# One x ring with paced chunk loads, a third product buffer and a second transpose bank in a dynamic convolution with mixture of depths

## The chip, the cores and the metric

One Trainium2 chip, one of its cores. TensorE (PE), VectorE (DVE), ScalarE (ACT), GpSimd (POOL) and SyncE (SP) run their own instructions in order and meet at semaphores. The metric is the device time of one execution in microseconds (us). Where several executions of a kernel are compared, their median is taken.

## What is computed

x is 8 x 4160 tokens of 192 values, weight_gen has 8 heads times 7 taps for each token. Part one is a causal convolution whose weights are a softmax over the 7 taps, for each token and head; part two takes, in each of the 8 sequences, the 128 tokens of the highest score and adds a gated two-layer expert to them:

```python
w = softmax(weight_gen, axis=-1)                      # (B, S, 8, 7)
x_pad = concat([zeros(6), x], axis=1)                 # along the tokens
out[b, s, h] = sum over k of w[b, s, h, k] * x_pad[b, s + k, h]
scores = out @ w_gate
for b in range(8):
    top = the 128 tokens of the highest scores[b]
    ye = relu(out[b, top] @ w1) @ w2                  # 192 -> 1024 -> 192
    out[b, top] += sigmoid(scores[b, top])[:, None] * ye
```

## The kernel before, in words

The 33,280 tokens are cut into 128 runs of 260, one for each partition. Each partition keeps its 260 tokens along the free dimension, and 6 more of the run before as a halo. The 260 are cut into 5 tiles of 52 tokens and 65 sub-steps of 4 tokens (13 a tile). Four tile buffers of x (fp16, converted by the load on POOL's queue, `load_x`, L593) exist; the fifth tile reuses the first.

Everything is emitted in one hand-written order, `phase`, and each engine runs its own instructions in that order. The main loop runs g from 0 to 65. In step g it emits:

- `products(g)`, L762 on VectorE: x of 10 tokens times the doubled weights, 5376 values a partition, written to a buffer of the pool `prodp` (two buffers).
- for each of two halves: a step of `softmax`, of `dots`, of `score`, of the selection, and `tap_sums(g - 1, half)`, L774: seven matmuls against the identity add up the taps of one half in PSUM.
- `store(g - 1)`: ScalarE copies the sums out (L782), SP's queue writes them (L783).

The generators are advanced by `next`, one piece of work for each call. `softmax` works on pieces of the weights: load on SP's queue (`load_wg`, L617, two pieces ahead, buffers shared with the halo), exponential on ScalarE into `e` (L649, three buffers), den by TensorE (L194), inverse by two ScalarE operations (L202, L204), each a call later, and the multiply on VectorE (L635). `dup_weights` (L746, ScalarE) writes each weight twice in a row for the products. `dots` computes x @ w_gate head by head for the scores: eight transposes on TensorE into the one bank `tps` (L697), a ScalarE copy `xT` (L702), eight small matmuls (L683) a call later, and a copy into `y16` (L688). The halo of each next tile is copied from the last (L605). `score` multiplies y with the weights (L719), sums the taps (L726) and reduces (L730).

When all tokens are scored, the selection starts: `threshold_selection` (top-8 of 260 scores, five times, then five rounds of a 15-way threshold search on VectorE and TensorE, then eight indirect loads of the picked list on POOL, L558), then `expert_pass`. That one computes the eight batches' picked rows anew: it gathers the 8 rows' weights (L253) and windows of x (L274, four ahead, and one for the head of the sequence, L279) with indirect loads on POOL, makes their softmax weights (es L295, den, inverse, we L304 and L308, wes L315), and then runs a loop over batches: `tap_rows` (L321), `conv_rows` (L334), `turn_rows` (L346), two `hidden` (L360, L364), `outputs` (L376) and `finish` (L383), a batch every three calls. From `rowf` on (a copy that waits for the picked list) the selection gets a call in both halves of a step, before that in one. At the end the eight batches are scattered into the output one after another (`scatter_rows`, L408): they write the tensor that the 65 stores wrote, and wait for these and for each other.

## Time and profile before

| | |
|---|---|
| median of 2 runs | 427.47 us (427.12 to 427.81) |
| the profiled execution | 424.73 us |
| its span, first to last instruction | 423.0 us |
| TensorE matmuls, busy | 251.7 us (60%) |
| VectorE, busy | 246.5 us (58%) |
| ScalarE, busy | 188.5 us (45%) |
| POOL, busy | 71.0 us (17%) |
| mean granted TensorE clock | 0.883 |
| products that start from 50.72, 151.62, 215.50, 286.02 and 321.02 us on | 12, 15, 13, 7 and 18 |

A busy time is the sum over the instructions of an engine. PE counts matmuls, whose ends are modelled; PEld (weight loads) overlaps with it. "[idle before <- releaser]" behind a row is the time that the engine stood still before it, and what ended that. The granted clock is 1.00 at 2.4 GHz and 0.50 at 1.2 GHz; between these it is a mean over both. GB/s counts the bytes as they land.

### The profile page before, as it was taken

How to read it: one execution, taken by the hardware profiler on the slowest of the kernel's cores; microseconds unless marked ns; L12 is line 12 of the kernel's file. 1: busy time of each engine (PE TensorE's matmuls, PEld its weight loads, DVE VectorE, ACT ScalarE, POOL GpSimd, SP SyncE). 2: the span in 40 equal slices, each digit the busy share in tenths (PEclk: the TensorE clock that was granted, in tenths of full speed). 3: DMA queues.
4: the chain of work that ended last, by engine and by line, in shares of the span. 5: the costliest groups of instructions: out<-in, count | busy, mean ns of one | idle time of the engine just before them, and what ended most of it. 6: DMA issues, size and time to landing. Idle time of an engine off the chain costs nothing. (4 is left out here: it accounts for less than half of the span.)

```text
span 423.0 us, 5356 instructions
## 1 busy us (share of the span) xinstructions
PE 251.7 (60%) x2174; PEld 159.8 (38%) x2174; DVE 246.5 (58%) x224; ACT 188.5 (45%) x244; POOL 71.0 (17%) x75
## 2 busy tenths in 40 slices
PE   0001117656466999799985757646267999996000
PEld 0001115333343666566642323323134777753000
DVE  1000242443435798687899999739529999894000
ACT  2004259656756785878723132204036666642000
POOL 3500000000000030000000000375847630000230
PEclk9999999886987999999998786886869999999555
DMA  8999974422311249921220211112149762224000
GB/s 139 238 244 230 242 212 141 162 93 81 104 69 40 77 110 230 240 113 77 114 113 37 115 74 75 63 52 112 56 84 239 152 174 103 113 112 154 29 28 20
DMA packets 17529, 51.41 MB, mean 122 GB/s; under 512 B 3989, under 2 KB 4379, under 8 KB 16346
## 3 DMA queue, kind: packets, MB, share of 16 engines
q0 software_dynamic: 5040, 17.35, 21.9%
q1 hardware_dynamic: 12458, 33.66, 21.5%
q8 instruction: 19, 0.31, 0.3%
q14 instruction: 12, 0.10, 0.1%
HBM read 41.61 MB, written 26.40 MB: 161 GB/s over the span
## 5 line engine op out<-in xcount | busy, mean ns | idle before, releaser
L762 DVE TENSOR_TENSOR prod<-xt,wd 128x5376 f16<-128x5376 f16 x65 | 191.5, 2954 | 77.5 <-PE cps L774 56.5
L774 PE MATMUL cps<-prod,ident 128*128 128x384 f16 x910 | 186.7, 355 | 27.0 <-DVE prod L762 24.7
L774 PEld LDWEIGHTS <-ident 128*128 128x128 f16 x910 | 90.5, 105 | 96.6 <-DVE prod L762 36.1
L782 ACT COPY co<-cps 128x768 f32<-128x768 f32 x65 | 51.9, 799 | 77.1 <-PE cps L774 62.1
L702 ACT COPY xT<-tps 128x1024 f16<-128x1024 f16 (+3 forms) x52 | 50.7, 975 | 15.2 <-PE tps L697 14.4
L649 ACT ACTIVATE e<-wg_t 128x896 f16<-128x896 f32 (+3 forms) x16 | 29.3, 1830 | 62.7 <-DMA wg_t<-in_weight_gen_dram 47.6
L194 PE MATMUL den<-e,ident 128*128 128x128 f16 (+3 forms) x112 | 11.6, 261 | 70.9 <-ACT lnd L202 66.4
L194 PEld LDWEIGHTS <-ident 128*128 128x128 f16 x119 | 10.4, 121 | 86.8 <-issue 83.5
L697 PE MATMUL tps<-ident,xt 128*128 128x128 f16 x399 | 33.1, 229 | 0.0
L558 POOL DMA_INDIRECT picked<-list_d,at_i x8 | 11.6, 1444 | 113.2 <-DVE flag L567 111.1
L683 PE MATMUL yps<-gmat,xT 128*128 128x8 f16 (+1 forms) x399 | 18.2, 169 | 19.2 <-ACT xT L702 18.8
L593 POOL DMA_DIRECT2D xt<-in_x_dram x11 | 6.2, 578 | 136.6 <-DVE scores L730 135.8
L683 PEld LDWEIGHTS <-xT 128*128 128x128 f16 x399 | 15.0, 98 | 33.2 <-ACT xT L702 32.4
L746 ACT COPY wd<-w 128x1792 f16<-128x1792 f16 (+3 forms) x16 | 27.4, 1710 | 0.0
L697 PEld LDWEIGHTS <-xt 128*128 128x128 f16 x399 | 24.6, 102 | 0.0
L274 POOL DMA_INDIRECT big<-in_x_dram,win_i x8 | 21.8, 2731 | 8.9 <-DVE big L321 7.6
L635 DVE TENSOR_TENSOR w<-e,r 128x896 f16<-128x896 f16 (+3 forms) x16 | 9.9, 627 | 22.3 <-ACT r L204 21.6
L408 POOL DMA_INDIRECT out_dram<-big,row_i x8 | 7.8, 978 | 64.3 <-DMA out_dram<-co 49.4
L253 POOL DMA_INDIRECT wsel<-in_weight_gen_dram,row_i x8 | 15.2, 1900 | 7.4 <-DVE win_i L222 5.3
L719 DVE TENSOR_TENSOR sp<-w,y 128x1344 f16<-128x1344 f16 (+3 forms) x10 | 9.1, 912 | 8.0 <-ACT y L688 8.0
L368 ACT ACTIVATE hT<-hps 128x512 bf16<-128x512 f32 x16 | 9.7, 605 | 6.5 <-PE hps L364 6.2
L831 DVE TENSOR_SCALAR xt<-halo,keep_p 128x1152 f16<-128x1152 f32 x1 | 0.8, 820 | 17.6 <-DMA halo<-in_x_dram 17.6
(130 smaller groups left out, 158.6 us busy)
## 6 DMA issues: line engine op xcount, KB each, us to landing
out_dram<-co SPq DMA_DIRECT2D x65, 384.0 KB, 2.3
xt<-in_x_dram POOLq DMA_DIRECT2D x8, 1248.0 KB, 22.2
wg_t<-in_weight_gen_dram SPq DMA_DIRECT2D x10, 448.0 KB, 7.2
wg_t<-in_weight_gen_dram SPq DMA_DIRECT2D x4, 560.0 KB, 3.6
xt<-in_x_dram POOLq DMA_DIRECT2D x1, 1344.0 KB, 16.4
xt<-in_x_dram POOLq DMA_DIRECT2D x1, 768.0 KB, 9.4
halo<-in_x_dram SPq DMA_DIRECT2D x1, 504.0 KB
xt<-in_x_dram POOLq DMA_DIRECT2D x1, 384.0 KB, 6.4
```

Of the source, the lines that this page charges most:

```text
L194: nc.tensor.matmul(out=den[:, :, :], lhsT=ident16[:, :], rhs=e_k(k), start=(k == 0), stop=(k == K - 1),)
L253: nc.gpsimd.indirect_dma_start(out=wsel[:, b, :], out_offset=None, in_=wg_flat[:, :], in_offset=bass.IndirectOffsetOnAxis(ap=row_i[:, b:b ...
L274: nc.gpsimd.indirect_dma_start(out=win_of(b), out_offset=None, in_=x_elems, in_offset=bass.IndirectOffsetOnAxis(ap=win_i[:, b:b + 1], axis=0),
L558: nc.gpsimd.indirect_dma_start(out=picked[:, b, :], out_offset=None, in_=list_d[:, :], in_offset=bass.IndirectOffsetOnAxis(ap=at_i[:, b:b ...
L649: nc.scalar.activation(out=es[n][:, :, :, :], in_=wgts[n].rearrange("p (s c) h k -> p s k (c h)", c=C), func=AF.Exp)
L683: nc.tensor.matmul(out=o, lhsT=lhs, rhs=m, start=(w == 0), stop=(w == 2), skip_group_check=True,)
L697: nc.tensor.transpose(out=tps[:, j, :], in_=xf[:, (r0 + j) * RUN:(r0 + j + 1) * RUN], identity=ident16[:, :],)
L702: nc.scalar.copy(out=xT[:, 0:m, :], in_=tps[:, 0:m, :])
L746: nc.scalar.copy(out=wd[:, 0:n, :, :, :], in_=w16s[it][:, s0:s0 + n, :, :, None].to_broadcast([P, n, K, CH, 2]),)
L762: nc.vector.tensor_tensor(out=prod.rearrange("p k t (h a b) -> p k t h a b", h=H, b=2), in0=xwin, in1=wd.rearrange("p k (c h) b -> p k c h ...
L774: nc.tensor.matmul(out=cps[:, j, 0:HB], lhsT=ident16[:, :], rhs=pf[:, k, j * HB:(j + 1) * HB], start=(k == 0), stop=(k == K - 1),)
L782: nc.scalar.copy(out=co[:, :, :], in_=cps[:, :, 0:HB])
```

## The change

The tiles of x become one ring of 168 tokens (and 6 of halo) in one buffer, filled by chunks: 8 and 16 tokens first, then 20 or so, each issued on POOL behind a tiny copy that reads the result of the n-th exponential (`after_exp`), the rest when the products of a certain step are emitted. All multiplied weights are kept in one tensor `w16`. Pieces of the weights are one sub-step, then four at a time, loaded three ahead into a pool of their own (three buffers); the halo has a product buffer. `e` has four buffers, `xT` three, `tps` two banks (a pool `ps2`, which the expert's `hps` uses as well), the products three buffers. In `softmax`, den and inverse stand in one call; in `dots`, the small matmuls come two calls behind their transposes. Dots get 0.82 calls a half from step 1 on; the selection starts at a first half. Scores are copied out of PSUM by ScalarE before the reduce. In `expert_pass` the row weights are gathered and made in two halves of four batches, between window gathers, and the loop handles a batch every two calls. The scatter stands inside `phase`, still last.

```diff
-    T = 52
-    NT = SP // T
+    RING = 168
...
+    ps2 = ctx.enter_context(tc.tile_pool(name="ps2", bufs=2, space=PSUM))
...
-        for b in range(NWIN):
-            gather(b)
+        for j in range(2):
+            for b in range(j * B // 2, (j + 1) * B // 2):
+                gather_weights(b)
+            for b in range(j * NWIN // 2, (j + 1) * NWIN // 2):
+                gather(b)
...
+        def row_weights(j):
+            h = slice(j * BH, (j + 1) * BH)
+            nc.scalar.activation(
+                out=es[:, h, :, :],
+                in_=wsel[:, h, :].rearrange("p b (h k) -> p b k h", k=K), func=AF.Exp
+            )
+            den = tap_sum(lambda k: es[:, h, k, :], BH, H)
+            rs = inverse(den, BH, H)
+            nc.vector.tensor_tensor(
+                out=we[:, h, :, :], in0=es[:, h, :, :],
+                in1=rs[:, :, None, :].to_broadcast([P, BH, K, H]), op=MUL,
+            )
...
         for _ in range(GWAIT):
             yield
...
+        row_weights(0)
+        yield
+        yield
+        double(0)
+        row_weights(1)
+        yield
         yield
...
-            tp = ps1.tile([P, 2, P], BF16, tag="tps", name="tp")
+            tp = ps1.tile([P, 2, P], BF16, tag="den", name="tp")
...
-            hps = ps1.tile([P, FC // 2, P], FP32, tag=("den", "sps")[half], name="hps")
+            hps = ps2.tile([P, FC // 2, P], FP32, tag="tps", name="hps")
...
-        for i in range(B + 4):
-            if 0 <= i - 3 < B:
-                finish(i - 3, outputs(i - 3))
+        for i in range(B + 3):
+            if 0 <= i - 1 < B:
+                conv_rows(i - 1)
             if i < B:
                 tap_rows(i)
+            if i == 0:
+                double(1)
             if 0 <= i - 2 < B:
                 hidden(i - 2, 0)
             yield
...
                 hidden(i - 2, 1)
-            yield
-            if i < B:
-                conv_rows(i)
+            if 0 <= i - 3 < B:
+                finish(i - 3, outputs(i - 3))
             yield
...
-        xin = cctx.enter_context(tc.tile_pool(name="xin", bufs=4))
-        xtp = cctx.enter_context(tc.tile_pool(name="xtp", bufs=2))
-        wfull = cctx.enter_context(tc.tile_pool(name="wfull", bufs=4))
-        ep = cctx.enter_context(tc.tile_pool(name="ep", bufs=3))
+        xin = cctx.enter_context(tc.tile_pool(name="xin", bufs=1))
+        xtp = cctx.enter_context(tc.tile_pool(name="xtp", bufs=3))
+        wgl = cctx.enter_context(tc.tile_pool(name="wgl", bufs=3))
+        ep = cctx.enter_context(tc.tile_pool(name="ep", bufs=4))
...
-        prodp = cctx.enter_context(tc.tile_pool(name="prodp", bufs=2))
+        prodp = cctx.enter_context(tc.tile_pool(name="prodp", bufs=3))
...
+        xr = xin.tile([P, RING + PAD, D], FP16, tag="xr", name="xr")
+        w16 = xin.tile([P, NSUB, K, CH], FP16, tag="w16", name="w16")
...
+        pieces = [(0, 1)] + [(a, a + 4) for a in range(1, NSUB, 4)]
...
+        def after_exp(n):
+            nc.gpsimd.tensor_copy(out=tick[:, n:n + 1], in_=es[n][0:1, 0, 0, 0:1])
...
-                j = n - 2
-                if 0 <= j < np_:
-                    rs[j] = inverse(dens[j], pieces[j][2] - pieces[j][1], CH)
                 j = n - 1
-                if 0 <= j < np_:
+                if 0 <= j < NP:
                     e = es[j]
-                    dens[j] = tap_sum(lambda k: e[:, :, k, :], pieces[j][2] - pieces[j][1], CH)
+                    m = pieces[j][1] - pieces[j][0]
+                    rs[j] = inverse(tap_sum(lambda k: e[:, :, k, :], m, CH), m, CH)
...
-                    if n + 2 < np_:
-                        load_wg(n + 2)
+                    if n + 3 < NP:
+                        load_wg(n + 3)
+                    if n in paced:
+                        after_exp(n)
+                        load_x(*paced[n])
...
-            for i in range(len(plan) + 1):
-                if i > 0:
+            for i in range(len(plan) + 2):
+                if i > 1:
...
-                    tps = ps1.tile([P, GRP, P], FP16, tag="tps", name="tps")
+                    tps = ps2.tile([P, GRP, P], FP16, tag="tps", name="tps")
...
-                sps = ps1.tile([P, m, CH], FP32, tag="sps", name="sps")
+                sps = ps1.tile([P, m, CH], FP32, tag="den", name="sps")
...
+                nc.scalar.copy(
+                    out=ss.rearrange("p s (c h) -> p s (c h)", c=C), in_=sps[:, :, :]
+                )
...
+        load_wg(1)
+        load_gate()
+        load_wg(2)
+        load_x(8, 24)
+        edges = [24, 44, 64, 84, 104, 124, 144, RING]
+        paced = dict(enumerate(zip(edges[:-1], edges[1:])))
...
         next(sm)
+        gate_matrix()
...
-        next(sm)
-        dup_weights(0, 0)
-
+        for _ in range(3):
+            next(sm)
+        dup_weights(0)
+
+        late = []
+        for a in range(RING, SP, 20):
+            b = min(SP, a + 20)
+            late.append(((b - RING + PAD - 1) // C + 1, a, b))
...
-                if g < 3 or half == 0:
+                if half == 0 and (g < 8 or g % 3):
                     advance(sm)
-                if g >= DOT0[min(NT - 1, state["block"])]:
-                    advance(dt)
+                if g >= 1:
+                    done_dots += DOTS
+                    if done_dots >= 1:
+                        done_dots -= 1
+                        advance(dt)
...
+            if late and g >= late[0][0]:
+                load_x(*late.pop(0)[1:])
...
-    GWAIT = 6
+    GWAIT = 4
+    DOTS = 0.82
```

## Rows read from the trace of the kernel before

**Rows 1.** By stage: window; its us; busy (count) by engine; clock; DMA share; GB/s.

```profile
0.00:50.72 50.72, 2.34 (x21) 2.01 (x22) 2.63 (x6) 8.88 (x11) 9.25 (x34) 1.00 0.98 217
50.72:151.62 100.90, 63.37 (x632) 42.69 (x632) 49.73 (x46) 65.92 (x83) 0.00 (x0) 0.88 0.36 112
151.62:215.50 63.88, 58.96 (x688) 39.94 (x685) 51.23 (x28) 48.37 (x55) 4.32 (x8) 1.00 0.54 146
215.50:286.02 70.52, 45.49 (x216) 22.35 (x215) 59.35 (x94) 16.14 (x19) 11.56 (x8) 0.81 0.19 74
286.02:321.02 35.00, 18.62 (x91) 9.56 (x91) 22.38 (x19) 11.41 (x16) 23.59 (x13) 0.75 0.40 107
321.02:385.60 64.58, 60.53 (x516) 42.00 (x516) 61.16 (x35) 36.48 (x64) 14.47 (x5) 1.00 0.50 142
385.60:423.00 37.40, 2.45 (x14) 1.29 (x14) 0.00 (x0) 1.31 (x2) 7.82 (x8) 0.59 0.12 44
```

**Rows 2.** Timeline, start: start, us, engine, line, operation [idle before, releaser].

```profile
21.89 0.82 DVE L831 TENSOR_SCALAR xt<-halo,keep_p 128x1152 f16<-128x1152 f32 x1 [17.55 <-DMA halo<-in_x_dram]
...
35.95 1.80 ACT L649 ACTIVATE e<-wg_t 128x896 f16<-128x896 f32 x1 [31.54 <-DMA wg_t<-in_weight_gen_dram]
...
48.46 1.40 ACT L649 ACTIVATE e<-wg_t 128x672 f16<-128x672 f32 x1 [8.11 <-DMA wg_t<-in_weight_gen_dram]
...
50.72 2.96 DVE L762 TENSOR_TENSOR prod<-xt,wd 128x5376 f16<-128x5376 f16 x1 [12.14 <-ACT wd L746]
```

**Rows 3.** Timeline, one step of the slow stage, and two later products.

```profile
118.74 2.96 DVE L762 TENSOR_TENSOR prod<-xt,wd 128x5376 f16<-128x5376 f16 x1 [3.20 <-PE cps L774]
...
121.62 0.62 DVE L635 TENSOR_TENSOR w<-e,r 128x896 f16<-128x896 f16 x1
...
122.27 1.80 ACT L649 ACTIVATE e<-wg_t 128x896 f16<-128x896 f32 x1 [2.15 <-DVE w L635]
123.98 0.99 ACT L702 COPY xT<-tps 128x1024 f16<-128x1024 f16 x1
...
125.69 2.09 PE L774 MATMUL cps<-prod,ident 128*128 128x384 f16 x7
...
127.82 2.96 DVE L762 TENSOR_TENSOR prod<-xt,wd 128x5376 f16<-128x5376 f16 x1 [5.24 <-PE cps L774]
...
137.53 2.88 DVE L762 TENSOR_TENSOR prod<-xt,wd 128x5376 f16<-128x5376 f16 x1
...
155.70 2.96 DVE L762 TENSOR_TENSOR prod<-xt,wd 128x5376 f16<-128x5376 f16 x1 [0.83 <-ACT xT L702]
```

**Rows 4.** Timeline, gathers and row weights after the selection.

```profile
290.78 3.25 POOL L253 DMA_INDIRECT wsel<-in_weight_gen_dram,row_i  x1 [0.30 <-DVE inside L245]
...
303.42 0.94 POOL L253 DMA_INDIRECT wsel<-in_weight_gen_dram,row_i  x1 [0.30 <-issue]
...
312.68 1.02 POOL L279 DMA_INDIRECT big<-xpad,head_i  x1 [4.54 <-issue]
...
318.40 3.54 POOL L274 DMA_INDIRECT big<-in_x_dram,win_i  x1 [0.30 <-issue]
...
321.02 0.85 DVE L321 TENSOR_TENSOR big<-big,wes 128x1344 f16<-128x1344 f16 x1
```

**Rows 5.** Timeline of TensorE in the row loop.

```profile
340.04 1.30 PE L774 MATMUL cps<-prod,ident 128*128 128x384 f16 x7
341.18 0.82 PE L376 MATMUL yep<-w_sb,hT 128*128 128x192 bf16 x8
...
346.83 0.82 PE L376 MATMUL yep<-w_sb,hT 128*128 128x192 bf16 x8
```

**Rows 6.** Timeline, the first and last of eight scatters.

```profile
392.52 1.02 POOL L408 DMA_INDIRECT out_dram<-big,row_i  x1 [49.38 <-DMA out_dram<-co]
...
414.29 0.97 POOL L408 DMA_INDIRECT out_dram<-big,row_i  x1 [2.15 <-issue]
```

More of the change, by code (lines that the diff above doesn't have):

```diff
@@ L251, in expert_pass, with gather_weights @@
         wsel = rowp.tile([P, B, HK], FP32, tag="wsel", name="wsel")
-        for b in range(B):
+        def gather_weights(b):
             nc.gpsimd.indirect_dma_start(
@@ new lines, in row_weights @@
+        def row_weights(j):
[10 more added lines that the diff above has]
+            )
+            nc.vector.tensor_tensor(
+                out=we[:, h, :, :], in0=we[:, h, :, :],
+                in1=inside[:, h, :, None].to_broadcast([P, BH, K, H]), op=MUL,
+            )
@@ L300, in expert_pass @@
-        yield
-        rs = inverse(den, B, H)
-        yield
-        we = rowp.tile([P, B, K, H], FP16, tag="we", name="we")
-        nc.vector.tensor_tensor(
-            out=we[:, :, :, :], in0=es[:, :, :, :],
-            in1=rs[:, :, None, :].to_broadcast([P, B, K, H]), op=MUL,
-        )
-        nc.vector.tensor_tensor(
-            out=we[:, :, :, :], in0=we[:, :, :, :],
-            in1=inside[:, :, :, None].to_broadcast([P, B, K, H]), op=MUL,
-        )
+        row_weights(0)
         yield
@@ L313, in expert_pass @@
         yield
-        wes = rowp.tile([P, B, K, H, 2], FP16, tag="wes", name="wes")
-        nc.scalar.copy(
-            out=wes[:, :, :, :, :], in_=we[:, :, :, :, None].to_broadcast([P, B, K, H, 2])
-        )
+        double(0)
+        row_weights(1)
+        yield
         yield
@@ L601, in new_x @@
-        def new_x():
-            xts.append(xin.tile([P, T + PAD, D], FP16, tag="xt", name=f"xt{len(xts)}"))
-        def halo_copy(it):
-            nc.scalar.copy(out=xts[it][:, 0:PAD, :], in_=xts[it - 1][:, T:T + PAD, :])
-        pieces = [(0, 0, 2), (0, 2, 6), (0, 6, 10), (0, 10, 13)]
-        for it in range(1, NT):
-            pieces += [(it, 0, 4), (it, 4, 8), (it, 8, 13)]
-        wgts = {}
+        xr = xin.tile([P, RING + PAD, D], FP16, tag="xr", name="xr")
+        xflat = xr.rearrange("p t d -> p (t d)")
@@ new lines, in phase, with load_x @@
+        w16 = xin.tile([P, NSUB, K, CH], FP16, tag="w16", name="w16")
+        def load_x(a, b):
+            o = PAD + a % RING
+            nc.gpsimd.dma_start(
+                out=xr[:, o:o + b - a, :],
+                in_=bass.AP(
+                    tensor=x_flat.tensor, offset=x_flat.offset + a * D,
+                    ap=[[SP * D, P], [D, b - a], [1, D]],
+                ),
+            )
+        pieces = [(0, 1)] + [(a, a + 4) for a in range(1, NSUB, 4)]
+        NP = len(pieces)
@@ L613, in load_wg @@
+        wgts, es = {}, {}
         def load_wg(n):
-            it, a, b = pieces[n]
-            m = b - a
-            wg_t = wgp.tile([P, m * C, H, K], FP32, tag="wg", name="wg_t")
+            a, b = pieces[n]
+            wg_t = wgl.tile([P, (b - a) * C, H, K], FP32, tag="wg", name="wg_t")
             nc.sync.dma_start(
@@ L814, in phase @@
             )
-        load_x(0, [8, 24, 52])
-        gate_matrix()
-        for _ in range(3):
-            new_x()
-            load_x(len(xts) - 1, [0, 26, 52])
+        load_wg(1)
[4 more added lines that the diff above has]
+        paced = dict(enumerate(zip(edges[:-1], edges[1:])))
         start_p = scp.tile([P, 1], FP32)
@@ L841, in phase, with advance @@
         dt, sc, sel = dots(), score(), None
-        def advance(gen, n=1):
-            for _ in range(n):
-                next(gen, None)
+        dup_at = {a - 1: n for n, (a, b) in enumerate(pieces) if n}
+        def advance(gen):
+            next(gen, None)
         prods = {}
-        for g in range(NT * NSUB + 1):
-            it, s = divmod(g, NSUB)
-            if g < NT * NSUB:
-                prods[g] = products(it, s)
+        done_dots = 0.0
+        for g in range(NSUB + 1):
+            if g < NSUB:
+                prods[g] = products(g)
@@ L861, in phase @@
                     advance(sel)
                 if half == 0:
-                    s2 = s + 1
-                    if (it, s2) in chunks:
-                        dup_weights(it, s2)
-                    elif s2 == NSUB and it + 1 < NT:
-                        dup_weights(it + 1, 0)
-                    if s == 9 and it + 1 < NT:
-                        halo_copy(it + 1)
+                    if g in dup_at:
+                        dup_weights(dup_at[g])
+                    if g == RING // C - 10:
+                        nc.scalar.copy(out=xr[:, 0:PAD, :], in_=xr[:, RING:RING + PAD, :])
```

184 lines of the change are left out of this document (83 added, 101 removed).

## Prediction

> **What bounds it now.** I began with busy time by stage [rows 1], cut where the character of the loop changes; a "step" is one sub-step g: one product (VectorE, L762) and the tap sums of the product before it. The reader should see that no engine is full on average and that each stage has its own limit. To 50.72 us there is no product, and the DMA share is 0.98. To 151.62: 12 steps of 8.4 us, no engine above 66%. To 215.50: 15 steps of 4.26, TensorE 92% busy. To 286.02: 13 steps of 5.42, VectorE 84%, selection beside the products. To 321.02: 7 steps of 5.0, VectorE 64%. To 385.60: 18 steps of 3.59, VectorE 95%. Then 37.40 us without a product.
>
> Next I read the timeline of the start [rows 2]. Two exponentials wait 31.54 and 8.11 us for weight loads; the halo is there at 21.89, yet the first product starts at 50.72. Four x tiles (208 tokens, 10.2 MB as fp16) are in flight, and 217 GB/s over 50.72 us are 11.0 MB: weights sit behind x.
>
> Third came one whole step of the slow stage [rows 3]. Read it as a ring: product, weight multiply, exponential (which waited 2.15 for the multiply), xT copy, tap sums, next product: 118.74 to 127.82, 9.08 us. Two product buffers, three e buffers and one transpose bank hand each engine its buffer only when the one before is through.
>
> **The change, part by part.** Counted from the loops: 50 dot groups need 52 advances at 1.64 a step (0.82 a half), so dots end in g=32, scoring in g=34, and the selection starts in g=35 instead of 27. It takes 29 steps (13 of threshold, 16 of row work) instead of 38 and ends in g=63, inside the 65 steps: nothing spills behind the loop.
>
> *Start.* A chunk of 20 tokens is 0.98 MB in SBUF, a weight piece of four sub-steps 0.46 MB. The first product needs the fourth exponential, and ahead of its weights stand 44 tokens of x (2.16 MB), halo (0.57) and the pieces (1.49 with its own): 4.2 MB at 217 GB/s are 19.4, plus 1.4 before the first x load: 21 us. Below, 15, if x yields; above, 31: the piece used at 48.46 was loaded behind the exponential that ended near 37.75, so it took 10.7. The gate loads move behind a piece on SP's queue, and gate_matrix, now behind chunk 24 to 44 on POOL, holds chunk 44 to 64 until they land. That delays x, which has slack, and leaves the DMA engines to the weights. The tick copies are one element each; behind one stands only the next x load, on purpose.
>
> *Steps 0 to 7.* The ring is cut at three places: product g waits for tap sums g-3, exponential n for multiply n-4, transposes i for xT i-2, each a step or so old. What is left is each engine's load and the DMA. Up to g=8 the DMA has 8.26 MB of x, 5.2 of weights, 0.57 of halo and 2.8 of stores, 16.8 MB: 78 us at 217 GB/s, so g=8 at 79 at the latest. From below: ScalarE had 65.92 us of work in 12 steps with as many exponentials, 5.5 a step, less 0.36 of a 1.0 us xT copy: 5.1, g=8 at 62. I take 5.8 a step, g=8 at 67.4, nearer the lower end, since the dots are at token 61 by then and the last chunks may still be on their way.
>
> *Steps 8 to 19*, two softmax pieces in three steps. The nearest row is the old loop with its last softmax parts, 137.53 to 155.70, four steps of 4.54 [rows 3]; below, VectorE's own: 2.96, two thirds of 0.62, and 0.37 of scoring (in the third stage VectorE had 3.42 a step, 0.46 above a product, at two groups): 3.7. I take 4.4, as the dots are fewer a step: g=20 at 120.2. *Steps 20 to 34*, no softmax: 4.26 was with two groups and two product buffers [rows 1]; VectorE alone has 3.3, TensorE 3.6 (3.93 a step at two groups, 58.96 over 15). I take 3.8: g=35 at 177.2.
>
> TensorE's clock: the granted clock was 1.00 where TensorE was 92% busy and 0.88 where it was 63% busy [rows 1]; at 125.69 a tap half took 2.09 us [rows 3], at 340.04 1.30 [rows 5]. TensorE's 4 us of work in a 5.8 us step is 70%, later near 90%, so I charge nothing beyond 5.8. The Trainium skill (TensorE: Matmul & The Clock Gate, Part 1: The HAM clock gate) says that the throttled state is the default and that activity lifts it, which speaks against early steps that wait for DMA. By that rule the first eight steps would take about 7.2 each and the sum be 11 us longer; the trace agrees that the clock falls where TensorE waits.
>
> *Selection, 35 to 47.* The threshold code is unchanged and bound by VectorE, 13 steps as before: 70.5, g=48 at 247.7.
>
> *Row weights, 48 to 52.* On POOL a gather issued under a product took 3.25 us, one beside an idle VectorE 0.94, 0.30 apart [rows 4]. The new order is weights 0 to 3, window 0 with its head, window 1, weights 4 to 7, windows 2 and 3. The instructions are the old ones in halves, but exponential, den, inverse and the VectorE multiplies now stand in one call, so VectorE waits for the gathers directly, where it ran out of product buffers before. From the start of product 48: product 2.96, index work 1.3, products 49 and 50, to 10.2 us. Weights 3 is issued at about 12 and landed at 14, plus 2 for the chain to the inverse: VectorE waits 6. Product 51 ends at 19.6. Meanwhile POOL does window 0, its head (which waits 4.54 for the landing [rows 4]) and window 1, to 21.7, then four weights at 1.25, landed at 28.4, plus 2: VectorE waits 11. After product 52 the first tap_rows starts at 35, just as now (286.02 to 321.02), though five products lie before it instead of seven. Bounds: 24 without the second wait, 45 with every gather at 3.25. Behind es on ScalarE stand copy-outs, behind den on TensorE tap sums; both have room before the row loop. g=52 is over at 282.7.
>
> *Row loop.* One batch a step instead of two in three steps. TensorE: a tap half 1.14 (340.04 to 341.18), one batch 5.65 - 3 x 1.14 = 2.23 (341.18 to 346.83) [rows 5], so 4.51 a step; VectorE 2.96, 0.85 and a shorter finish, under 4.4. Products 53 to 64 are five full steps at 4.55, six that fill or drain at 3.3 to 4.2 (22.9), and the last product, 2.95: 48.6, to 331.3. Windows are gathered four batches ahead.
>
> *Tail.* Scatters still follow all stores and each other, 392.52 to 414.29 [rows 6]: the stage stays 37.4, to 368.7.
>
> *Costed at nothing.* The ring spares ScalarE three halo copies, where it isn't the bound. The ss copy, eight times on ScalarE, shares the den bank: a TensorE wait that 4.4 and 3.8 have room for. Late chunks wait on POOL for products, with selection masks, expert weights and, much later, gathers behind them, and are issued five or more steps (20 us) ahead of use. Could a chunk into the one ring tile hold up products on other tokens? Tap_rows at 321.02 ran while a gather into another part of big was still being issued (318.40 plus 3.54) [rows 4], so ranges are told apart. Keeping all weights issues nothing.
>
> The sum: 21 + 46.4 + 52.8 + 57 + 70.5 + 35 + 48.6 + 37.4 = 368.7 against a span of 423.0. The profiled execution is 424.73, so 1.7 lies around it: 370.4. The median of 427.47 is 2.7 above that execution: 373.
>
> **Rivals.** *Weights still late.* The DMA stays full to g=8, which comes at 79, and the ring empties more slowly up to g=20: 385 to 397. For it: a wait of 31.54 behind x now. Against: one chunk for each exponential. Chance 0.2.
> *Cold TensorE.* If the granted clock stays low through the first 20 steps, twice 3.6 is 7.2 a step: +45, 418. Against: a TensorE that is the bound is always busy, and the stage from 151.62 had 1.00. Chance 0.08.
> *The ring survives*, the other side. The inverse now stands in the call of its own den, so ScalarE waits for TensorE before its exponential. If that closes a new ring, the 20 softmax steps keep a length like the old one: at 8.1 a step the time is 436, at 9.08 it is 455. From 8.1 on the change is slower. Against: den is TensorE's first work of a step, on an input a step old. Chance 0.05.
> *More hides*: 3.8 and 3.4 a step in 8 to 34 (-13) and no second wait in the row weights (-11): 349. For it: beside an idle VectorE, POOL runs at 1.25. Chance 0.15.
>
> **How the numbers follow.** My own case has 0.52 and its own range is 356 to 390 (start 15 to 31, g=8 at 62 to 79, row weights 24 to 45, not all at one end). With the late weights above and the better case below the range is 346 to 402, which leaves out about 0.15. Less than 2% either way (419 to 436) is about what can't be told from no change. Faster: my case, the late weights, the better case and part of the cold TensorE, 0.89; the rest of that, 0.06, within; the surviving ring 0.05.
>
> **What would show it.** First product near 21 us; spacing of products near 5.8, 4.4 and 3.8 where it was 8.4 and 4.26; no wait of VectorE for tap sums before g=35; the first top-8 near 181; waits of 6 and 11 us on VectorE for the inverse, about g=51 and 52; spacing near 4.5 in the row loop with TensorE full; the tail at 37.4. I am wrong if steps 0 to 19 keep 8 us, if exponentials still wait for weights after g=8, or if rows finish behind the last product.

## Result and the profile after

The changed kernel takes 378.33 us (median of 2 runs, 377.89 to 378.77) beside 427.47: a ratio of 0.885 [0.880, 0.890]. Forecast were 373 and a range of 346 to 402. The profiled execution took 378.77 us, its span is 377.1, the mean granted clock 0.886.

Busy time by stage of the changed kernel, the view of [rows 1]. The cuts are the starts of products 0, 8, 20, 35 and 48, the end of product 52, and the end of product 64:

```profile
0.00:27.32 27.32, 2.59 (x26) 2.29 (x27) 2.43 (x7) 9.12 (x12) 5.74 (x24) 1.00 0.84 199
27.32:72.43 45.11, 29.99 (x268) 20.36 (x266) 28.66 (x18) 31.31 (x39) 8.15 (x19) 0.89 0.95 247
72.43:136.40 63.97, 51.56 (x604) 37.60 (x602) 44.68 (x39) 50.16 (x65) 4.27 (x8) 0.97 0.62 167
136.40:188.37 51.97, 50.95 (x568) 36.45 (x567) 49.34 (x27) 40.14 (x50) 1.06 (x2) 1.00 0.48 145
188.37:258.42 70.05, 42.73 (x209) 20.80 (x209) 58.71 (x93) 15.28 (x18) 11.94 (x8) 0.87 0.20 74
258.42:291.04 32.62, 14.33 (x63) 6.94 (x64) 16.96 (x20) 9.46 (x17) 17.32 (x13) 0.66 0.44 97
291.04:337.92 46.88, 46.00 (x437) 34.64 (x436) 43.69 (x28) 28.32 (x56) 13.42 (x4) 1.00 0.49 132
337.92:377.10 39.18, 3.24 (x20) 1.75 (x18) 0.00 (x0) 1.60 (x2) 7.83 (x8) 0.60 0.14 52
```

The reader should see two things. The first eight steps are 5.64 us each and the next twelve 5.33, where the first twelve were 8.4. And in the third row no engine is above 81% of 63.97 us, so something other than an engine's load still sets those steps. In the fourth row TensorE has 98%, and that stage has a bound.

By the starts of products, 23.4 us are gained at product 0 (50.72 to 27.32), 53.0 at product 12, 70.7 at product 35 and 66.3 at product 48. Behind it 18.5 are given back: steps 48 to 63 take 76.55 us instead of 58.0, since the selection now starts at step 35 and its row weights and row loop both lie there. The span is 45.9 shorter.

The start, timeline of ScalarE and VectorE, answering [rows 2]:

```profile
18.43 1.80 ACT L660 ACTIVATE e<-wg_t 128x896 f16<-128x896 f32 x1 [14.03 <-DMA wg_t<-in_weight_gen_dram]
...
21.75 1.78 ACT L660 ACTIVATE e<-wg_t 128x896 f16<-128x896 f32 x1
24.52 0.28 ACT L203 ACTIVATE lnd<-den 128x128 f32<-128x128 f32 x1 [0.99 <-PE den L195]
...
25.05 1.78 ACT L660 ACTIVATE e<-wg_t 128x896 f16<-128x896 f32 x1
26.73 0.55 ACT L763 COPY wd<-w 128x448 f16<-128x448 f16 x1
...
27.32 2.96 DVE L778 TENSOR_TENSOR prod<-xr,wd 128x5376 f16<-128x5376 f16 x1 [10.62 <-ACT wd L763]
```

Weights are there at 18.43, for the second exponential, and the two behind it do not wait for theirs; before, exponentials waited until 35.95 and 48.46. But the exponentials then follow each other 3.3 us apart, each behind the den and inverse of the one before, and the doubling of piece 0, whose own exponential was done at 3.5, stands behind all three.

Waits of the changed kernel over the span (engine, line, releaser: us, times, longest):

```profile
DVE prod L778 <- ACT wd L763: 38.7, 10, 10.6
ACT r L205 <- DVE w L647: 18.2, 7, 3.8
ACT e L660 <- DMA wg_t<-in_weight_gen_dram: 18.0, 4, 14.0
DVE we L310 <- ACT r L205: 15.4, 2, 10.2
```

No product waits for tap sums any more, where such waits of 3.20 and 5.24 us stood in [rows 3]. VectorE now waits for the doubled weights, and ScalarE, before it can write an inverse `r`, for a weight multiply. One such turn in steps 9 to 12, timeline of both engines:

```profile
81.04 1.69 ACT L763 COPY wd<-w 128x1792 f16<-128x1792 f16 x1
82.75 2.96 DVE L778 TENSOR_TENSOR prod<-xr,wd 128x5376 f16<-128x5376 f16 x1 [6.83 <-ACT wd L763]
...
86.63 2.95 DVE L778 TENSOR_TENSOR prod<-xr,wd 128x5376 f16<-128x5376 f16 x1
89.50 0.62 DVE L647 TENSOR_TENSOR w<-e,r 128x896 f16<-128x896 f16 x1
90.21 0.31 ACT L205 ACTIVATE r<-lnd 128x128 f16<-128x128 f32 x1 [3.81 <-DVE w L647]
...
98.77 0.31 ACT L205 ACTIVATE r<-lnd 128x128 f16<-128x128 f32 x1 [3.59 <-DVE w L647]
```

`r` has two buffers. The multiply reads `r` two calls after it is written, so the inverse of piece n+2 can only be written when the multiply of piece n is through. That multiply stands behind a product on VectorE, and the product behind a doubling on ScalarE. It is a ring through two engines, smaller than the old one.

Row weights, timelines of POOL and VectorE, answering [rows 4]; and TensorE at the end of the row loop, answering [rows 5]:

```profile
262.66 5.82 DVE L778 TENSOR_TENSOR prod<-xr,wd 128x5376 f16<-128x5376 f16 x2
263.18 3.24 POOL L255 DMA_INDIRECT wsel<-in_weight_gen_dram,row_i  x1 [0.30 <-issue]
266.73 2.57 POOL L255 DMA_INDIRECT wsel<-in_weight_gen_dram,row_i  x1 [0.31 <-issue]
269.61 0.94 POOL L255 DMA_INDIRECT wsel<-in_weight_gen_dram,row_i  x1 [0.30 <-issue]
...
273.66 0.28 DVE L310 TENSOR_TENSOR we<-es,r 128x224 f16<-128x224 f16 x1 [5.18 <-ACT r L205]
...
276.18 1.95 POOL L282 DMA_INDIRECT xr<-xpad,head_i  x1 [4.36 <-issue]
...
287.46 0.28 DVE L310 TENSOR_TENSOR we<-es,r 128x224 f16<-128x224 f16 x1 [10.24 <-ACT r L205]
...
290.95 0.85 DVE L337 TENSOR_TENSOR xr<-xr,wes 128x1344 f16<-128x1344 f16 x1
...
333.51 0.82 PE L392 MATMUL yep<-w_sb,hT 128*128 128x192 bf16 x8
334.17 6.99 PE L790 MATMUL cps<-prod,ident 128*128 128x384 f16 x42
```

The two forecast waits of VectorE are there (5.18 and 10.24 us). In the last row, 3.75 us before the last product ends (at 337.92), TensorE still has 42 matmuls in front of it: six tap halves, or three products.

### The profile page after: what moved, and what is told of

Same layout as the page of the kernel before. It is cut to its first block, busy times and chain, and to the rows that moved or that the text cites. A ratio compares the mean times of both kernels' runs of the same rounds, so it can differ in the third digit from the quotient of the medians.

```text
span 377.1 us, 5393 instructions
## 1 busy us (share of the span) xinstructions
PE 241.4 (64%) x2181; PEld 160.8 (43%) x2181; DVE 244.5 (65%) x225; ACT 185.4 (49%) x255; POOL 69.7 (18%) x85
## 3 DMA queue, kind: packets, MB, share of 16 engines
q1 hardware_dynamic: 12602, 33.66, 23.5%
## 5 line engine op out<-in xcount | busy, mean ns | idle before, releaser
L778 DVE TENSOR_TENSOR prod<-xr,wd 128x5376 f16<-128x5376 f16 x65 | 191.1, 2949 | 38.7 <-ACT wd L763 38.7
L719 ACT COPY xT<-tps 128x1024 f16<-128x1024 f16 (+1 forms) x50 | 50.2, 1012 | 6.5 <-PE tps L715 6.0
L660 ACT ACTIVATE e<-wg_t 128x896 f16<-128x896 f32 (+1 forms) x17 | 29.5, 1738 | 18.0 <-DMA wg_t<-in_weight_gen_dram 18.0
L195 PE MATMUL den<-e,ident 128*128 128x128 f16 (+1 forms) x119 | 11.3, 248 | 37.9 <-ACT e L660 35.1
L195 PEld LDWEIGHTS <-ident 128*128 128x128 f16 x133 | 10.3, 113 | 56.8 <-issue 52.8
L715 PE MATMUL tps<-ident,xr 128*128 128x128 f16 x399 | 32.1, 226 | 0.0
L763 ACT COPY wd<-w 128x1792 f16<-128x1792 f16 (+1 forms) x17 | 27.6, 1623 | 0.0
L715 PEld LDWEIGHTS <-xr 128*128 128x128 f16 x399 | 24.2, 101 | 0.3 <-issue 0.3
L277 POOL DMA_INDIRECT xr<-in_x_dram,win_i x8 | 17.3, 2158 | 7.2 <-DVE xr L337 6.0
L425 POOL DMA_INDIRECT out_dram<-xr,row_i x8 | 7.8, 979 | 54.5 <-issue 48.2
L205 ACT ACTIVATE r<-lnd 128x128 f16<-128x128 f32 (+1 forms) x19 | 5.6, 297 | 18.5 <-DVE w L647 18.2
L736 DVE TENSOR_TENSOR sp<-w,y 128x1792 f16<-128x1792 f16 (+2 forms) x9 | 9.0, 995 | 4.6 <-ACT y L705 4.6
```

Of the source, the lines that this page charges most:

```text
L195: nc.tensor.matmul(out=den[:, :, :], lhsT=ident16[:, :], rhs=e_k(k), start=(k == 0), stop=(k == K - 1),)
L277: nc.gpsimd.indirect_dma_start(out=win_of(b), out_offset=None, in_=x_elems, in_offset=bass.IndirectOffsetOnAxis(ap=win_i[:, b:b + 1], axis=0),
L660: nc.scalar.activation(out=es[n][:, :, :, :], in_=wgts[n].rearrange("p (s c) h k -> p s k (c h)", c=C), func=AF.Exp)
L715: nc.tensor.transpose(out=tps[:, j, :], in_=xflat[:, e0:e0 + RUN], identity=ident16[:, :],)
L719: nc.scalar.copy(out=xT[:, 0:m, :], in_=tps[:, 0:m, :])
L763: nc.scalar.copy(out=wd[:, 0:b - a, :, :, :], in_=w16[:, a:b, :, :, None].to_broadcast([P, b - a, K, CH, 2]),)
```

## Experiments

Each was timed beside the kernel before on the same chip (medians there 427.2 to 429.2 us). Starts of products in each kernel's own profile, in us:

| kernel | time | ratio | p 0 | p 8 | p 20 | p 35 | p 48 | p 64 |
|---|---|---|---|---|---|---|---|---|
| before | 427.5 | 1 | 50.7 | 127.8 | 186.7 | 259.1 | 324.7 | 382.7 |
| changed | 378.3 | 0.885 | 27.3 | 72.4 | 136.4 | 188.4 | 258.4 | 335.0 |
| u1_two_products | 396.7 | 0.927 | | 79.5 | 143.5 | 197.1 | | 354.2 |
| u5_old_buffers | 420.4 | 0.982 | | 87.2 | 166.4 | 223.0 | | |
| u2_x_at_once | 399.7 | 0.932 | 50.8 | 92.0 | 156.3 | 208.3 | | |
| b1_start_alone | 422.0 | 0.983 | 31.6 | 122.6 | 182.9 | | | |
| u3_four_inverses | 367.9 | 0.860 | 28.1 | 73.7 | 126.7 | 178.7 | | |
| u4_double_earlier | 372.8 | 0.873 | | 71.6 | 129.9 | 181.8 | | |
| r1_window_first | 377.0 | 0.880 | | | | | 258.3 | |
| v1_three_edits | 364.7 | 0.849 | 27.6 | 73.0 | 125.8 | 176.8 | 246.9 | 321.0 |
| s1_start | 378.6 | 0.884 | 17.1 | 71.6 | 135.6 | 187.5 | 257.8 | 334.3 |
| s2_spread | 363.0 | 0.848 | 27.7 | 69.1 | 119.9 | 175.0 | 245.2 | 319.2 |
| s3_spread_start | 362.5 | 0.849 | 17.4 | 69.1 | 119.8 | 175.0 | 244.1 | 318.1 |
| w1_four_stores | 356.4 | 0.835 | 28.1 | 63.2 | 113.1 | 168.2 | 237.2 | 311.2 |

### Is it the buffers? One undone, then all

```diff
-        prodp = cctx.enter_context(tc.tile_pool(name="prodp", bufs=3))
+        prodp = cctx.enter_context(tc.tile_pool(name="prodp", bufs=2))
```

> The changed kernel with two product buffers instead of three. Theory A (the third buffer takes TensorE out of VectorE's way): VectorE waits for tap sums again, steps 20 to 34 take about 4.2 us instead of 3.46 (+11), the steps before them 0.3 to 0.5 more each (+8), the row loop some more; total 392 to 402. Rival B (ScalarE's doubling is what holds the products, the third buffer fills and empties without use): total 378 to 384.

Measured: 396.7 us [0.920, 0.934], 18.4 above the changed kernel. Products wait 25.8 us for tap sums again, 23 times. The loss is not where one would look first: 7 us by product 8, none from 8 to 20 and 1.6 from 20 to 35, the other 10 behind product 35, nearly all in the row weights and the row loop (7.28 and 4.54 us a step where the changed kernel has 6.66 and 3.93). The third buffer pays little in steps 20 to 34, where TensorE is simply full.

```diff
-    ps2 = ctx.enter_context(tc.tile_pool(name="ps2", bufs=2, space=PSUM))
+    ps2 = ctx.enter_context(tc.tile_pool(name="ps2", bufs=1, space=PSUM))
...
-        xtp = cctx.enter_context(tc.tile_pool(name="xtp", bufs=3))
+        xtp = cctx.enter_context(tc.tile_pool(name="xtp", bufs=2))
...
-        ep = cctx.enter_context(tc.tile_pool(name="ep", bufs=4))
+        ep = cctx.enter_context(tc.tile_pool(name="ep", bufs=3))
...
-        prodp = cctx.enter_context(tc.tile_pool(name="prodp", bufs=3))
+        prodp = cctx.enter_context(tc.tile_pool(name="prodp", bufs=2))
...
-            for i in range(len(plan) + 2):
+            for i in range(len(plan) + 1):
...
-                        lhs = xTs[i - 2][:, r - r0, :]
+                        lhs = xTs[i - 1][:, r - r0, :]
```

> The changed kernel with the old buffer counts at all three cuts of the ring: two products, three e, one transpose bank with xT two deep and the dots one call behind; chunks stay paced. (The one bank also serves the expert's hidden sums, so the row loop is slower for a second reason; read steps 0 to 34 alone.) Theory A (the ring product, multiply, exponential, xT copy, tap sums set the slow stage): the softmax steps go back to 7.5 to 9 us, g=20 comes 40 to 70 us later than 136.4, total 420 to 450. Rival B (the slow stage was slow because weights came late, and pacing cured that): g=20 moves by less than 15 us, total 385 to 398.

Measured: 420.4 us [0.975, 0.990]. The waits of products for tap sums over the whole span, in the kernel before and in this one:

```profile
DVE prod L762 <- PE cps L774: 56.5, 25, 12.0
DVE prod L778 <- PE cps L790: 56.3, 24, 6.6
```

With the ring of x, the paced loads and the kept weights all in place, the old buffers give back 42 of the 49 us. Of these 35 are lost by product 35; 6 lie in the row loop, where the one bank also holds the expert's hidden sums, which neither of the other two kernels asks of one bank. By product 20 they have cost 30: theory A had 40 to 70 and rival B less than 15, so the total is theory A's and the size is not. No exponential waits for weights once the products run (both such waits, 14.7 us, lie ahead of product 0), so this is the ring without late weights. The steps from 20 to 34 stay near the changed kernel's (3.77 and 3.46 us). Of the three cuts only the third product buffer was undone alone: it has 7.1 of the 30 us (u1_two_products); the `e` buffers and the bank with `xT` were not.

### Is it the loads? Pacing undone, then alone in the old kernel

```diff
+        for a, b in zip(edges[:-1], edges[1:]):
+            load_x(a, b)
-        paced = dict(enumerate(zip(edges[:-1], edges[1:])))
+        paced = {}
```

> The changed kernel with all chunks of the ring (168 tokens) issued on POOL at once at the start, none behind an exponential. Theory A (pacing lets the weights past x): the HW queue gets a small share while x is in flight, as before the change; product 0 comes at 38 to 48 us instead of 27.3, g=8 at 78 to 88 instead of 72.4, total 384 to 394. Rival B (the DMA has the same bytes to move up to g=8 either way, and that sets g=8): product 0 later, g=8 within 4 us of 72.4, total 376 to 382.

Measured: 399.7 us [0.929, 0.936], 21.4 above the changed kernel (20.0 by the ratios) and more than theory A had. Timeline of ScalarE and VectorE in its start:

```profile
21.49 1.80 ACT L660 ACTIVATE e<-wg_t 128x896 f16<-128x896 f32 x1 [17.00 <-DMA wg_t<-in_weight_gen_dram]
42.10 1.80 ACT L660 ACTIVATE e<-wg_t 128x896 f16<-128x896 f32 x1 [17.20 <-DMA wg_t<-in_weight_gen_dram]
48.54 1.80 ACT L660 ACTIVATE e<-wg_t 128x896 f16<-128x896 f32 x1 [3.03 <-DMA wg_t<-in_weight_gen_dram]
50.82 2.96 DVE L778 TENSOR_TENSOR prod<-xr,wd 128x5376 f16<-128x5376 f16 x1 [34.00 <-ACT wd L763]
```

That is [rows 2] over again: product 0 at 50.82 where it was at 50.72. The 23.5 us lost there are 19.6 at product 8 and 20 from then on.

In the kernel before, with the halo in a product buffer, weights of piece 1 ahead of the gate's, and the second to fourth tile of x in halves behind exponentials:

```diff
-            load_x(len(xts) - 1, [0, 26, 52])
+        for i in range(1, 4):
+            for cuts in ([0, 26], [26, 52]):
+                paced[len(paced)] = (i, cuts)
...
+                    if n in paced:
+                        nc.gpsimd.tensor_copy(
+                            out=tick[:, n:n + 1], in_=es[n][0:1, 0, 0, 0:1]
+                        )
+                        load_x(*paced[n])
```

> The kernel before with only the start of the change: the halo in a product buffer, the second weight piece issued ahead of the gate loads, and the half tiles of x tiles 1 to 3 (26 tokens each) issued on POOL behind the first six exponentials. Buffers, dots, selection and row work as before. Theory A (start and ring are two separate losses): product 0 near 30 us, and the 12 steps after it keep 8 to 9 us; total 402 to 410. Rival B (the slow steps were slow because weights came late): these steps fall to 5 to 6 us as well, total 370 to 385.

Measured: 422.0 us [0.979, 0.986]; product 0 19 us earlier, product 8 5 us, product 20 4 us. Neither theory had this. The 12 steps from product 0 on take 9.7 us each, where the kernel before has 8.4 and theory A had 8 to 9, and in them exponentials wait 19.1 us for weights, where they waited 6.6 before. So this pacing moves part of the late weights behind product 0, and the run alone cannot tell the ring from late weights. One turn of its slow stage, timeline of all engines:

```profile
83.35 2.96 DVE L769 TENSOR_TENSOR prod<-xt,wd 128x5376 f16<-128x5376 f16 x1 [2.19 <-PE cps L781]
...
86.22 0.62 DVE L637 TENSOR_TENSOR w<-e,r 128x896 f16<-128x896 f16 x1
86.87 1.80 ACT L651 ACTIVATE e<-wg_t 128x896 f16<-128x896 f32 x1 [2.15 <-DVE w L637]
90.67 2.35 PE L781 MATMUL cps<-prod,ident 128*128 128x384 f16 x7
93.06 2.96 DVE L769 TENSOR_TENSOR prod<-xt,wd 128x5376 f16<-128x5376 f16 x1 [5.99 <-PE cps L781]
```

The ring of [rows 3] in 9.71 us, with the same 2.15 us at the exponential. The parts of the change are worth more together than alone: this pacing in the old kernel 7 us (429.2 on that chip to 422.0), everything else of the change without pacing 29 (429.2 to 399.7), all of it 49. In the new kernel, undoing the pacing costs 21 (378.3 to 399.7) and undoing the buffers 42 (378.3 to 420.4). By product 20, where the changed kernel is 50.3 us ahead, the two cost 19.9 and 30.0.

One gap stays open. b1_start_alone and u5_old_buffers both have paced loads and old buffers, and yet product 20 comes at 182.9 in the one and at 166.4 in the other. What differs there (finer chunks, other pieces, weights asked for three pieces ahead, den and inverse in one call, fewer dots a step) was not tried part by part.

### Why are steps 8 to 19 longer than forecast? The small ring of `r`

```diff
-    wgp = ctx.enter_context(tc.tile_pool(name="wgp", bufs=2))
+    wgp = ctx.enter_context(tc.tile_pool(name="wgp", bufs=4))
```

> The changed kernel with four buffers instead of two for the inverse r (and its logarithm). In the changed kernel ScalarE stands 18.2 us, seven times, in front of r for the weight multiply that frees the r buffer, 11.2 of it in steps 8 to 19, which took 5.33 us each where 4.4 were predicted. Theory A (these steps are short of ScalarE time, and the wait is part of it): the wait is gone, g=20 comes 8 to 12 us earlier, total 366 to 371. Rival B (the wait lies beside another, the next engine is as late): the wait is gone, the total moves by less than 3 us, 375 to 379.

Measured: 367.9 us [0.854, 0.866], 10.4 below the changed kernel. Its third stage, busy time by stage, beside the changed kernel's third row above:

```profile
73.66:126.65 52.99, 49.16 (x601) 36.30 (x599) 44.38 (x39) 49.76 (x65) 4.26 (x8) 1.00 0.76 202
```

The same work in 52.99 us instead of 63.97, 4.42 a step, and nothing gained before product 8 or behind product 20. The wait of `r` for the multiply is gone from the list. One buffer count, of a pool with two small tiles (`r` and its logarithm `lnd`), was worth a fifth of what the whole change brought. It is `r` that counts: w1_four_stores below has `lnd` back at two, and its steps 8 to 19 take 4.16 us.

```diff
-        dup_at = {a - 1: n for n, (a, b) in enumerate(pieces) if n}
+        dup_at = {max(0, a - 2): n for n, (a, b) in enumerate(pieces) if n}
```

> The changed kernel with each doubling of the weights (but the first two) issued one step earlier on ScalarE. VectorE waits 38.7 us for the doubling in ten products, 10.6 of it before product 0 and 3.7 before product 1, which this leaves as they are. Theory A (the doubling is late because ScalarE reaches it last in the step in which it is needed): the other 24 us of waits shrink to under 8, g=20 comes 8 to 14 us earlier, total 364 to 370. Rival B (ScalarE is full in these steps, an earlier doubling pushes the exponentials and copies back): total within 3 us of 378.

Measured: 372.8 us [0.867, 0.880]. Products wait 21.9 us for the doubled weights instead of 38.7, and the stage is 58.3 us. This opens the same ring at another point and gets half of u3's gain there, between the two theories; ScalarE's wait for `r` falls from 18.2 to 12.7 us.

### Row weights: window 0 first

```diff
-        for j in range(2):
-            for b in range(j * B // 2, (j + 1) * B // 2):
-                gather_weights(b)
-            for b in range(j * NWIN // 2, (j + 1) * NWIN // 2):
-                gather(b)
+        gather(0)
+        for b in range(B // 2):
+            gather_weights(b)
+        gather_head(0)
+        for b in range(B // 2, B):
+            gather_weights(b)
+        for b in range(1, NWIN):
+            gather(b)
```

> The changed kernel with another order of the gathers on POOL: window 0, weights 0 to 3, its head, weights 4 to 7, windows 1 to 3. In the changed kernel POOL stands 4.36 us for the landing of window 0 before its head, with weights 4 to 7 behind, and VectorE waits 5.18 and 10.24 us for the inverses. Theory A (the second wait is POOL's order): the first wait grows to 6 to 8, the second falls to 4 to 6, the row loop starts 3 to 5 us earlier, total 373 to 375. Rival B (window 0's bytes delay the weights' landing as much): no change, 377 to 379.

Measured: 377.0 us [0.875, 0.884], within 1.4 us of the changed kernel, which its spread can't tell from none. VectorE's timeline does tell it:

```profile
276.05 0.28 DVE L315 TENSOR_TENSOR we<-es,r 128x224 f16<-128x224 f16 x1 [7.67 <-ACT r L205]
...
284.94 0.28 DVE L315 TENSOR_TENSOR we<-es,r 128x224 f16<-128x224 f16 x1 [5.32 <-ACT r L205]
...
288.43 0.85 DVE L342 TENSOR_TENSOR xr<-xr,wes 128x1344 f16<-128x1344 f16 x1
```

The head no longer stands before four weight gathers; the first wait grows by 2.5 and the second falls by 4.9, as theory A had it, and the row loop starts 2.5 us earlier, less than its 3 to 5.

> The changed kernel with four inverse buffers, the doubling a step earlier and the gather order of r1_window_first together. Alone the first gave 367.9, the second 372.8 us against 378.3. Theory A (the waits for r and for the doubling are two faces of ScalarE's time in steps 0 to 19): together little more than the better one, 364 to 367, and 3 to 5 less from the gathers: 360 to 364. Rival B (they add up): 10.4 + 5.5 + 4: 357 to 359.

The three edits together: 364.7 us [0.844, 0.854], just above theory A's 360 to 364. Steps 8 to 19 take 4.40 us each where u3_four_inverses alone has 4.42: the earlier doubling adds nothing to it, as two openings of one ring would have it. The rest of the gain on u3_four_inverses, 3 us, lies in steps 20 to 34 (3.40 us each instead of 3.47) and the row weights.

### Does the start count?

```diff
+                if n == 1:
+                    nc.vector.tensor_tensor(
+                        out=w16[:, 0:1, :, :], in0=es[0][:, :, :, :],
+                        in1=rs[0][:, :, None, :].to_broadcast([P, 1, K, CH]), op=MUL,
+                    )
...
+                    dup_weights(0)
...
-        dup_weights(0)
```

(gate_matrix moves behind product 0.)

> The changed kernel with only its start reordered: the weights of piece 0 are multiplied and doubled right behind their inverse, ahead of exponential 1, and the gate matrix is built behind product 0. Product 0 then waits for the halo (15.7 us) and not for three exponentials behind the weights that land at 18.4: it should start at 16.5 to 18 in place of 27.3. Theory A, the start of product 0 is a term of the sum: its 9 to 10 us arrive at product 8 with at least 5 left, time 368 to 373. Theory B, the first stage ends when its transfers do (the DMA engines are 0.94 busy from product 0 to product 8, and doubling 1 still stands behind exponential 4, so product 1 starts at 31 to 34): product 8 within 2 us of 72.4, product 20 within 2 of 136.4, time 376 to 380. Above 381 neither holds.

Measured: 378.6 us [0.880, 0.888], nothing gained. VectorE's timeline:

```profile
17.05 2.96 DVE L785 TENSOR_TENSOR prod<-xr,wd 128x5376 f16<-128x5376 f16 x1
...
32.69 2.96 DVE L785 TENSOR_TENSOR prod<-xr,wd 128x5376 f16<-128x5376 f16 x1 [9.27 <-ACT wd L770]
```

Product 0 comes 10.3 us earlier, product 1 only 1.8 and product 8 only 0.8. The numbers of theory B came. Its reason, that transfers end the stage, is tried further down: s2_spread takes transfers out of these steps and so cannot tell; w1_four_stores keeps all that s2_spread has.

```diff
-                if half == 0 and (g < 8 or g % 3):
+                if half == 0 and (g < 4 or g % 2):
                     advance(sm)
```

> The kernel of v1_three_edits (364.7 us, product 8 at 73.0, product 20 at 125.8) with the softmax pieces taken at every step only to step 3 and at every second step from there, so that its last weight load goes out some 8 steps later. Theory A, in steps 4 to 7 the exponentials stand on ScalarE waiting for weights that no product needs for a dozen steps (7.3 us at the exponentials, 16.5 us at the products for the doubled weights behind them), and their loads take the DMA engines from x: product 8 at 64 to 70, and a few tenths are given back in steps 20 to 26, time 357 to 362. Theory B, x itself is late in that stage whatever the weights do: product 8 at 72 to 74, time 363 to 366. Theory C, what leaves the early steps comes back after step 20, where TensorE already fills the steps: product 8 earlier, product 35 not, 363 to 367. A selection that starts later than in v1_three_edits (product 48 less than 68 us behind product 35) would show as time above 367.

Measured, on top of v1_three_edits: 363.0 us [0.844, 0.852]. Product 8 comes 4.0 us earlier (69.1, inside theory A), product 20 5.9, but product 35 only 1.8: steps 20 to 34 take 3.68 us with the last pieces in them instead of 3.40. The total lies at the lower end of theory C's 363 to 367. With the new start on top:

> The kernel of s2_spread with the start of s1_start as well. Theory A of both: product 0 at 17 and, with fewer weight loads beside x, product 8 at 58 to 65, time 350 to 358. If the first stage is bound by its transfers (theory B of s1_start), product 8 lies within 2 us of that of s2_spread and the time within 2 us of it.

362.5 us [0.843, 0.855], product 8 at the same 69.1: product 0 again doesn't count. What s2_spread left in steps 4 to 7 is a copy on ScalarE. Its timeline:

```profile
51.10 1.84 ACT L724 COPY xT<-tps 128x896 f16<-128x896 f16 x2
58.28 0.80 ACT L803 COPY co<-cps 128x768 f32<-128x768 f32 x1 [5.34 <-DMA out_dram<-co]
58.97 0.28 ACT L203 ACTIVATE lnd<-den 128x128 f32<-128x128 f32 x1
...
61.19 0.31 ACT L710 CAST y<-yps 128x208 f16<-128x208 f32 x1
```

The copy needs a buffer whose store has not left yet; behind it on ScalarE stand an inverse, an exponential and the copy of y, for which the score multiply waits, and behind that product 6.

```diff
-        outp = cctx.enter_context(tc.tile_pool(name="outp", bufs=3))
+        outp = cctx.enter_context(tc.tile_pool(name="outp", bufs=4))
```

(`r` keeps its four buffers in a pool of its own, `lnd` has two again, which makes the room.)

> The kernel of s2_spread (363.0 us) with a fourth buffer for the convolution's rows on their way out (the inverses keep four buffers and their logarithms two). In s2_spread the copy of step 4's sums stood 5.3 us on ScalarE until a store had left (52.9 to 58.3 us), and the copy of y, the score multiply and products 6 and 7 stood behind it. Theory A, that ring is what is late next in steps 4 to 7: the wait falls below 2 us, product 6 starts at 56 to 59 in place of 62.2, product 8 at 64 to 67 in place of 69.1, time 358.5 to 361.5. Theory B, the DMA engines are what is late there (0.88 to 1.02 busy from 40 to 72 us) and the store's buffer is only where it shows: another transfer is waited for in its place (weights or x), product 8 at 68 to 70, time 362 to 364.

Measured: 356.4 us [0.831, 0.839], 6.5 below s2_spread (5.7 by the ratios), more than theory A had. Product 8 starts at 63.2, 5.9 us earlier. Timeline of ScalarE and one row by stage:

```profile
52.70 0.84 ACT L804 COPY co<-cps 128x768 f32<-128x768 f32 x1
...
55.65 0.31 ACT L711 CAST y<-yps 128x208 f16<-128x208 f32 x1
...
27.50:69.00 41.50, 30.67 (x335) 21.39 (x335) 31.38 (x18) 34.22 (x43) 9.20 (x20) 1.00 1.03 272
```

The copy runs 5.6 us earlier and doesn't wait. In the same window s2_spread has a DMA share of 0.97 and 249 GB/s where this row has 1.03 and 272, and a granted clock of 0.88 where this row has 1.00; TensorE did nothing from 56 to 59 us in s2_spread and worked on here, and some of the gain may be the clock's. The program asks for the same transfers in the same order, so transfers alone did not set the end of that stage in s2_spread, full as the DMA engines looked. This kernel is the fastest of the study, 22 us below the changed one.

## Why the prediction was right, and where it was not

The direction, the mechanism and the total held: 373 forecast, 378.33 measured. The span is 8.4 us above the sum of 368.7, and the terms miss by more than that in both directions:

| term | forecast | measured | difference |
|---|---|---|---|
| start | 21 | 27.32 | +6.3 |
| steps 0 to 7 | 46.4 | 45.11 | -1.3 |
| steps 8 to 19 | 52.8 | 63.97 | +11.2 |
| steps 20 to 34 | 57 | 51.97 | -5.0 |
| selection | 70.5 | 70.05 | -0.4 |
| row weights | 35 | 32.62 | -2.4 |
| row loop | 48.6 | 46.88 | -1.7 |
| tail | 37.4 | 39.18 | +1.8 |

Of the 8.4, 2.7 are offset by the step from the profiled execution to the median, which the prediction added, and 0.4 by the median after, which lies below its profiled execution: 5.3 remain. The total is nearer than its terms by luck: they miss by about 19 us one way and 11 the other, and nothing in the prediction ties the two.

- **The ring is cut**: right, and shown by u5_old_buffers, which brings it back with the weights on time (56.3 us of waits for tap sums, 56.5 before, none in the changed kernel). b1_start_alone shows the same turn in the old kernel, but beside late weights. That the loads had to be paced as well was right, too: u2_x_at_once loses 20 us by product 8 and keeps that loss. The prediction did not say that the parts are worth less alone.
- **Steps 8 to 19**, the step that failed: "What is left is each engine's load and the DMA." I listed three places where the ring was cut and did not look for the buffers that stayed at two. The forecast of 4.4 us a step was right for a kernel without that ring: u3_four_inverses has 4.42.
- **Start**: sized from bytes, it had all weights up to the fourth exponential's landed by 20.8 (19.4 and 1.4), and the trace bears that out as far as it goes: the second exponential starts at 18.43 and the next two wait for none. It left out the three exponentials 3.3 us apart that stand before the doubling. The miss cost nothing, though: s1_start takes it away and the time stays. The start and steps 0 to 7 are not two terms but one, which ended at 72.43 where 67.4 was forecast, inside the bounds of 62 and 79 (the upper one came from 217 GB/s; the stage landed 247). What ended it can be said in part: behind v1_three_edits, with `r` at four buffers, weights asked for long before their use and a store that had not left held up ScalarE's queue, and with both eased the stage ended at 63.2. In the changed kernel's own steps 0 to 7 ScalarE waits 7.0 us for the multiply that frees `r`, 3.1 for weights and only 1.0 for a store. What each of these is worth at product 8 there was not tried; u3_four_inverses, which takes the first away, gains nothing by product 8.
- **Steps 20 to 34**: TensorE's 3.6 was the bound, as the prediction listed it, and the measured 3.46 is nearer to it than the 3.8 that I took; the allowance for anything else was not needed. Beside u1_two_products (3.57 a step), the third buffer has little part in it.
- **Row weights and row loop**: the waits of 6 and 11 us came as 5.18 and 10.24, and the row loop 1.7 us shorter. r1_window_first shows that the order of the gathers shares these waits out (7.67 and 5.32 us, 2.4 less in all); their number was not varied.
- **Tail**: with three product buffers VectorE can run further ahead of TensorE, so tap sums of three products are left at 334.17. TensorE has 3.24 us of work behind the last product where it had 2.45 [rows 1], and the first scatter is issued 8.2 us behind that product instead of 6.9; the eight scatters take 21.7 us from first to last issue as in [rows 6]. The other 0.6 us lie behind the last of them. In u1_two_products, with two product buffers, the first scatter is issued 7.4 us behind the last product.
- **The clock**: nothing was charged, rightly. It was granted at 0.89 in steps 0 to 7, with TensorE busy 66% of them, then at 0.97 and 1.00. The rule of the Trainium skill that the prediction weighed (TensorE: Matmul & The Clock Gate, Part 1: The HAM clock gate) would have made those steps 7.2 us; they took 5.64.
- **The rivals**: weights were not late (product 8 at 72.4, not 79), and no exponential waited for one after product 8 in the changed kernel. The surviving ring came in a milder form than the prediction priced: not through TensorE's den, but through VectorE's multiply, 0.9 us a step instead of 2.3 or more.

## What to carry to other kernels

When a ring is cut by adding buffers, list every tile pool on its way, the smallest too, and compare its buffers with the calls between write and last read: the ring closes again at the next pool that is one short. An engine that runs in order waits at the head of its queue for everybody behind; a copy-out that waits for a store, or an exponential for weights needed a dozen steps later, stalls what is urgent. Before a stage's first event is worked on, ask what sets its last one: ten microseconds at product 0 were worth 0.8 at product 8.

## What was not expected of the hardware

- A DMA share near 1 stood beside very different rates: in w1_four_stores it was 1.00 at 227 GB/s from 55 to 57 us and 1.03 at 415 GB/s from 61 to 63 us. And a mean hides its course: the 0.95 of the changed kernel's steps 0 to 7 is 1.02 to 1.03 up to 60 us and 0.76 from there to product 8, so the DMA engines had room when that stage ended.
- A gather on POOL issued under a product ends some 0.8 us behind that product: 263.18 plus 3.24 and 266.73 plus 2.57 are 0.8 to 0.9 behind the ends of products 49 and 50, and beside an idle VectorE the gather at 269.61 takes 0.94. The Trainium skill (SBUF — State Buffer, Who interferes with whom) has it that VectorE and GpSimd share a pair of ports, and that a VectorE instruction with two inputs in SBUF contends with a GpSimd instruction that reads SBUF. These rows agree as far as POOL's waiting goes: a product has two inputs, and a gather reads its row numbers `row_i`. That the ports are what POOL waits for is not shown.
